# Projecting every token chunk with the activations as TensorE weights

## The chip, the cores and the metric

The kernel runs on one core of one Trainium2 chip. Its metric is the device time in microseconds (us) of one execution. TensorE (PE in the profile, PEld for its weight loads), VectorE (DVE), ScalarE (ACT), GpSimd (POOL) and the DMA queues of SyncE (SP), ACT and POOL run side by side, each through its own list of instructions in a fixed order, and wait for one another by semaphores.

## The reference

Two stages follow one another: a linear attention with a second-order feature map, and a feed-forward layer with a rational activation.

```python
# q, k, v: [4, 4, 1088, 32] (batch, head, sequence, head_dim); S1, S2: [8, 32]
def phi(x):                                   # 64 features per token and head
    a = einsum('rd,bhsd->bhsr', S1, x)
    b = einsum('rd,bhsd->bhsr', S2, x)
    return einsum('bhsi,bhsj->bhsij', a, b).reshape(..., 64)
q_p, k_p = phi(q), phi(k)
kv = einsum('bhsf,bhsd->bhfd', k_p, v)
z  = k_p.sum(axis=2)
x  = einsum('bhsf,bhfd->bhsd', q_p, kv) / (einsum('bhsf,bhf->bhs', q_p, z)[..., None] + 1e-6)
x  = x.transpose(0, 2, 1, 3).reshape(4352, 128)
# w_in: [128, 2048], w_out: [2048, 128], a: [4], b: [2]
h = x @ w_in
P = a[0] + a[1]*h + a[2]*h**2 + a[3]*h**3
Q = 1 + abs(b[0])*abs(h) + abs(b[1])*h**2
out = (P / (Q + 1e-6)) @ w_out                # [4352, 128], float32
```

## The kernel before

**Tiling.** The 4352 tokens are cut into ten chunks. The 4 x 1024 tokens of the main part give chunk `0` (128 tokens), chunk `0b` (384) and chunks `1` to `7` (512 each); the last 64 tokens of the four batches together are chunk `8` (256 tokens, the remainder). In the code `n` counts them from 0 to 9, and `lab(n)` gives the label. The 2048 hidden units are 16 blocks of 128 (`fi`). A group is one chunk with some of its blocks: chunk `0` has groups 0, 1, 2 (4, 4 and 8 blocks), chunk `0b` groups 3 and 4, chunks `1` to `7` two groups of 8 blocks each (5 to 18), the remainder groups 19 to 22 (8, 4, 3 and 1 blocks).

**One group** (`add_group`). TensorE computes `h` in float32 into `h_ps` (two buffers); ACT, and for some groups DVE, copies it to bf16 (`hev`, tile `hb`). DVE forms |h| (`abs`, tile `u`) and h squared (`sq`, tile `lin`). Q is u plus lin (`+Q`), added by an accumulating DMA of the POOL queue for groups 3 to 19 and by DVE otherwise. ACT takes the logarithm (`ln`, tile `L`) and the exponential of its negative (`exp`, back to `u`), which gives 1/Q. DVE builds the numerator in `y` (`odd`, `oddt`, then `+P`, by DMA or DVE) and multiplies it by 1/Q (`n5`). TensorE projects `y` with `w_out_b` into one PSUM bank, `out_ps` (`py`); for groups 11 to 22, whose plan has a "z", it also projects 1/Q itself with `w_out_0` (`pr`).

**The projection** (`project`). For nine of the ten chunks the weights are a 128x128 block of `w_out` and the chunk's `y` columns move (L891): 16 matmuls a chunk, or 32 with `pr`. The result lies with the output features on the partitions. So ACT copies it to SBUF (`oev`, L896, tile `o_sb`), TensorE transposes it in blocks of 128 tokens (`otr`, L901), ACT copies the transposes to `oT` (`otev`, L906), and SP stores that. The remainder alone (`BY_TOKEN = (9,)`) goes by tokens: a 128-token block of `y` is the weights and a block of `w_out` moves, 128 columns (L886); the result has tokens on the partitions, and one copy (L962) takes it to `oT`.

**Attention.** `add_keys(b)` makes the key features and the sums over them for batch b (`k tr`, `k ab`, `k prod`, `kv`, ...); `add_queries(n)` makes the chunk's attention output `xT` (`q tr`, `q abc`, `q dpr`: product for the denominator, `q prod`, `qp tr`, `x mm`, `x ev`). They share three PSUM buffers `w_ps` with `otr` and with the zeros below.

**Zeros.** `hot` multiplies zeros by zeros on TensorE, 23 matmuls of 512 columns in nine steps of `HOT` sizes (L1054), without effect on the output.

**Order.** Every piece is a step of `Plan`, with its engine, what it comes after, and the buffers that it takes and gives. `ORDER` is a list of the step numbers, written out, in which the steps are issued; each engine runs its share of them in that order. The costs given to `plan.add` have no effect while `ORDER` stands.

Of the kernel before, what the change touches and what calls it, by code (L numbers as in the profile page):

```python
# [55 lines left out]


class Plan:
# [66 lines left out]
def kernel(  # L125
# [14 lines left out]
    B, H, S, D = q.shape  # L140
# [7 lines left out]
    REM = S - MAIN  # L148
    JC = 4
    CW = JC * 128  # L150
# [9 lines left out]
    PLANS = {**{g: "QP" for g in range(4, 20)}, **{g:"QPz" for g in range(11,20)},5:"QP",3:"Q",4:"sQP",17:"Qz",20:"z",21:"z",22:"z"}  # L160
    CASTS = {18:(6,),16:(6,),14:(6,),12:(6,),17:(6,),13:(6,),15:(6,),11:(6,),10:(6,),9:(6,),8:(6,),7:(6,)}
    PACKED = (0, 9)
    BY_TOKEN = (9,)
    HOT = [1, 1, 1, 1, 5, 4, 6, 2, 2]
    ZEROS = 8
    assert d_model == 128 and H == 4 and D == 32 and R == 8 and REM == 64 and J % JC == 0

# [15 lines left out]
    plan = Plan(BUFS)  # L183
# [422 lines left out]
    def lab(n):  # L606
        return n - 1 if n > 1 else ("0", "0b")[n]
# [179 lines left out]
    def add_group(g, G):  # L787
        W, fis, n, how = G["W"], G["fis"], G["n"], G["how"]
        gw = W * len(fis)
        step = W if CW % W == 0 else CW  # L790
        subs = [(i, min(1024 // W, len(fis) - i)) for i in range(0, len(fis), 1024 // W)]
        by_token = n in BY_TOKEN
        final = fis[-1] == NF - 1
# [21 lines left out]
        def take(kind):  # L815
            return [] if packed else [KINDS[kind][0]]

        def got(kind):
            return [T[kind, "got", n]] if packed else []
# [88 lines left out]

        hes = []
        for s, nsub in subs:  # L910
            at = s * W // CW if W > B * REM or not by_token else s
            hm = plan.add("PE", 858 * nsub * W // 512, lambda s=s, w=nsub: h_mm(s, w), after=[G["x_step"], ld["wi"]], rank=g - 1.45,
                          take=["h_ps"], give=["xT"] if final and (s, nsub) == subs[-1] else [], name=f"h {g},{at}")
            dve = s in G["casts"]
            hes.append(plan.add("DVE" if dve else "ACT", 72 + nsub * W * 1.045 if dve else 32 + nsub * W * 0.853,
                                lambda s=s, w=nsub, e=nc.vector.tensor_copy if dve else nc.scalar.copy: h_evac(s, w, e), after=[hm] + got("t") + hes[:1], rank=g - 1.45,
                                take=take("t") if s == 0 else [], give=["h_ps"], name=f"hev {g},{at}"))
        pw = W // 128 * 85 if by_token else W / 2.4 + 3
        ts, tt = gw / 3.84 + 68, gw / 1.92 + 68

        def add_up(name, dst, src, after, rank, give=()):
# [23 lines left out]
        if z:  # L945
            rt = plan.add("PE", len(fis) * pw, lambda: project("u", w_out_0, first, False),
                          after=[e, rt] + c_w0[:1 + (fis[-1] >= NF // 2)], rank=g + 0.45, take=["out_ps"] if first else [], name=f"pr {g}")
# [11 lines left out]
        if final and by_token:  # L959
            def o_tokens():  # L960
                T["oT", n] = tile_of(moe, "oT", [128, JC, d_model], FP)
                nc.scalar.copy(out=T["oT", n][:, :W // 128, :],  # L962
                               in_=T["o", n][:, :W].rearrange("p (n d) -> p n d", d=d_model))

            t = plan.add("ACT", 32 + W * 109 // 128, o_tokens, after=[o], rank=g + 0.57, take=["oT"], give=["out_ps"],
                         name=f"otev {lab(n)}")
            t = plan.add("SP", 650, lambda: G["store"](T["oT", n]), after=[t], rank=g + 0.6, name=f"store {lab(n)}")
            plan.add("ST", 1, lambda: None, after=[t], rank=g + 0.6, give=["oT"], name=f"stored {lab(n)}")
        elif final:
            ev = 32 + W * 109 // 128  # L970
            o = plan.add("ACT", ev, o_evac, after=[o], rank=g + 0.56, take=["o_sb"], give=["out_ps"], name=f"oev {lab(n)}")
            t = plan.add("PE", 110 * (W // 128), o_transposes, after=[o], rank=g + 0.57, take=["w_ps"], give=["o_sb"],
                         name=f"otr {lab(n)}")
            t = plan.add("ACT", ev, oT_evac, after=[t], rank=g + 0.57, take=["oT"], give=["w_ps"], name=f"otev {lab(n)}")
            t = plan.add("SP", 650, lambda: G["store"](T["oT", n]), after=[t], rank=g + 0.6, name=f"store {lab(n)}")
            plan.add("ST", 1, lambda: None, after=[t], rank=g + 0.6, give=["oT"], lag=700, name=f"stored {lab(n)}")
# [32 lines left out]
    for n in range(len(chunks) + 1):  # L1009

        rank = first_of[n] - 2.6
        if n < len(chunks):
# [5 lines left out]
            def srcs(b=b, c=c, j0=j0, nj=nj):  # L1018
# [13 lines left out]
                give=["kq"] if c == NCH - 1 else [], early=early, pair=c if b > 0 else None)  # L1032
# [57 lines left out]
```

## Time and profile before

| what | value |
|---|---|
| median of 3 runs (lowest, highest) | 246.5 us (246.37, 246.71) |
| the profiled execution, its own time | 246.79 us |
| span, first to last instruction, in that execution | 244.8 us |
| PE busy | 237.0 us (97%), 1138 instructions |
| PEld busy | 137.0 us (56%), 1138 instructions |
| DVE busy | 223.8 us (91%), 241 instructions |
| ACT busy | 219.4 us (90%), 198 instructions |
| POOL busy | 50.1 us (20%), 70 instructions |
| mean granted TensorE clock | 0.998 |

A profile shows one execution. Busy time is the time in which an engine had at least one instruction under way; the modelled ends of pipelined matmuls overlap the next ones, so that for PE the distance from start to start says what a matmul costs. Engines are listed by line of the kernel (L891), with the tile written, an arrow and the tiles read. A figure in square brackets behind a row of a timeline is the time that the engine sat idle before it, and who ended that. The execution's own time is 2.0 us above its span.

### The profile page before, as it was taken

What the parts mean: (1) busy time and instruction counts of PE and PEld (TensorE: products, weight loads), DVE (VectorE), ACT (ScalarE), POOL (GpSimd) and SP (SyncE); (2) the same over time, 40 slices, a digit from 0 to 9 for tenths busy, and PEclk for the clock granted to TensorE, in tenths of its full rate; (3) what the DMA queues carried; (4) which work ended last, traced back from release to release, by engine and by line L of the source; (5) the groups of instructions that cost most, each with busy time, mean ns of one, the idle gap of its engine ahead of it and who ended that gap; (6) DMA issues with size and microseconds to landing.
All of it is one profiled execution on the core that took longest, in us unless ns stands there. A gap on an engine that the chain in (4) does not pass through costs nothing.

```text
span 244.8 us, 3043 instructions
## 1 busy us (share of the span) xinstructions
PE 237.0 (97%) x1138; PEld 137.0 (56%) x1138; DVE 223.8 (91%) x241; ACT 219.4 (90%) x198; POOL 50.1 (20%) x70
## 2 busy tenths in 40 slices
PE   8999999999999999999999999999999999999983
PEld 4888676655566555554554655344344444655452
DVE  0759969999999999999999999999999998999992
ACT  3337998998899979999999999999999999999993
POOL 7800020104021505030121420212211113111100
PEclk9999999999999999999999999999999999999999
DMA  6996716668959799989999899999999999999912
GB/s 165 277 319 170 255 22 111 166 135 196 188 99 185 126 183 181 188 158 191 205 173 184 151 212 187 187 209 183 189 189 215 185 175 181 203 190 179 194 43 67
DMA packets 22207, 42.96 MB, mean 175 GB/s; under 512 B 5537, under 2 KB 12721, under 8 KB 22065
## 3 DMA queue, kind: packets, MB, share of 16 engines
q0 software_dynamic: 8544, 31.74, 72.5%
q1 hardware_dynamic: 13360, 10.95, 14.9%
q8 instruction: 9, 0.15, 0.2%
q10 hardware_dynamic: 288, 0.08, 0.2%
q14 instruction: 6, 0.04, 0.0%
HBM read 8.82 MB, written 2.23 MB: 45 GB/s over the span
## 4 chain that ended last, share of the span: by engine, by line
PE 81%; DVE 8%; DMA 4%; ACT 4%; issue 2%; SPq 0%; DVEq 0%; ACTq 0%
PE h_ps L834 44%; PE out_ps L891 11%; PE w_ps L501 7%; DVE y L871 4%; PE w_ps L688 3%; PE w_ps L630 3%; PE w_ps L464 3%; PE w_ps L676 3%; DMA u<-lin 3%; PE w_ps L620 2%; ACT L L875 2%; DMA kq<-in_k_dram 2%; ACT u L878 2%; PE w_ps L455 1%; DVE lin L861 1%
## 5 line engine op out<-in xcount | busy, mean ns | idle before, releaser
L834 PE MATMUL h_ps<-xT,w_in_sb 128*128 128x512 f32 (+3 forms) x320 | 127.4, 534 | 0.0
L834 PEld LDWEIGHTS h_ps<-xT,w_in_sb 128*128 128x128 f32 x320 | 55.2, 190 | 42.1 <-issue 32.4
L875 ACT ACTIVATE L<-u,kappa 128x4096 f32<-128x4096 bf16 (+6 forms) x23 | 65.9, 2866 | 0.2 <-DMA u<-lin 0.2
L878 ACT ACTIVATE u<-L 128x4096 bf16<-128x4096 f32 (+6 forms) x23 | 63.7, 2769 | 0.1
L841 ACT CAST hb<-h_ps 128x1024 bf16<-128x1024 f32 (+3 forms) x52 | 52.1, 1022 | 5.1 <-PE h_ps L834 4.9
L927 POOL DMA_DIRECT2D u<-lin x17 | 21.1, 1241 | 115.8 <-DVE u L853 42.2
L871 DVE TENSOR_TENSOR y<-y,u 128x4096 bf16<-128x4096 bf16 (+6 forms) x23 | 39.6, 1727 | 1.1 <-ACT u L878 1.1
L871 DVE TENSOR_TENSOR y<-y,hb 128x4096 bf16<-128x4096 bf16 (+6 forms) x23 | 39.6, 1728 | 0.1
L861 DVE TENSOR_TENSOR lin<-hb 128x4096 bf16<-128x4096 bf16 (+6 forms) x22 | 38.0, 1728 | 0.7 <-ACT hb L841 0.6
L927 POOL DMA_DIRECT2D y<-lin x15 | 20.6, 1370 | 61.6 <-DVE lin L868 19.8
L891 PE MATMUL out_ps<-y,w_out_b 128*128 128x512 bf16 (+2 forms) x144 | 30.6, 355 | 0.9 <-DVE y L871 0.9
L865 DVE TENSOR_SCALAR y<-lin,a_t 128x4096 bf16<-128x4096 bf16 (+6 forms) x23 | 25.0, 1089 | 1.1 <-PE out_ps L891 0.9
L891 PEld LDWEIGHTS <-w_out_b 128*128 128x128 bf16 x144 | 13.3, 98 | 20.2 <-issue 7.9
L853 DVE TENSOR_SCALAR u<-hb 128x4096 int16<-128x4096 int16 (+6 forms) x23 | 21.6, 941 | 0.3 <-ACT hb L841 0.2
L891 PE MATMUL out_ps<-u,w_out 128*128 128x512 bf16 x64 | 15.1, 379 | 0.0
L841 DVE CAST hb<-h_ps 128x1024 bf16<-128x1024 f32 x12 | 14.6, 1214 | 0.0
L501 PEld LDWEIGHTS w_ps<-v_aug,k_p 128*128 128x128 f32 x112 | 13.4, 192 | 1.3 <-issue 1.0
L501 PE MATMUL w_ps<-v_aug,k_p 128*128 128x96 f32 x112 | 13.7, 274 | 0.0
L484 DVE TENSOR_TENSOR k_p<-ab 128x1024 f32<-128x1024 f32 x7 | 8.6, 1231 | 3.9 <-ACT q_pT L682 2.3
L891 PEld LDWEIGHTS <-w_out 128*128 128x128 bf16 x64 | 6.2, 98 | 8.4 <-issue 2.3
L868 DVE TENSOR_SCALAR lin<-lin,a_t 128x4096 bf16<-128x4096 bf16 (+3 forms) x11 | 10.9, 989 | 0.0
L676 PEld LDWEIGHTS w_ps<-ident,q_p 128*128 128x128 f32 x66 | 8.1, 141 | 5.0 <-issue 4.6
(121 smaller groups left out, 230.5 us busy)
## 6 DMA issues: line engine op xcount, KB each, us to landing
u<-lin POOLq DMA_DIRECT2D x14, 1024.0 KB, 9.4
y<-lin POOLq DMA_DIRECT2D x13, 1024.0 KB, 9.8
v_aug<-in_v_dram SPq DMA_DIRECT2D x8, 256.0 KB, 5.0
out_dram<-oT SPq DMA_DIRECT2D x7, 256.0 KB, 4.7
kq<-in_k_dram SPq DMA_DIRECT2D x3, 512.0 KB, 4.3
kq<-in_q_dram SPq DMA_DIRECT2D x3, 512.0 KB, 6.3
u<-lin POOLq DMA_DIRECT2D x2, 768.0 KB, 8.0
w_in_sb<-in_moe_w_in_dram SPq DMA_DIRECT2D x1, 1024.0 KB, 5.6
```

Source lines behind the costliest of these rows:

```text
L501: nc.tensor.matmul(kv_of((hp,))[:, 0], lhsT=lhs(hp), rhs=rhs(hp), start=(first and hp == hps[0]), stop=final, skip_group_check=True)
L676: nc.tensor.transpose(T["qpTp", n, hp][:, i * 128:(i + 1) * 128], in_=qp[:, i, hp * 128:(hp + 1) * 128], identity=ident)
L834: nc.tensor.matmul(T["h", g, s][:, i * step:i * step + W], lhsT=w_in_sb[:, fi * 128:(fi + 1) * 128], rhs=T["xT", n][:, :W], start=True, st ...
L841: copy(out=T["t", g][:, s * W:(s + nsub) * W], in_=T["h", g, s][:, :nsub * W])
L853: nc.vector.tensor_scalar(out=u().bitcast(mybir.dt.int16), in0=ht().bitcast(mybir.dt.int16), scalar1=0x7FFF, scalar2=None, op0=AX.bitwise_and)
L861: nc.vector.tensor_mul(out=sq(), in0=ht(), in1=ht())
L865: nc.vector.tensor_scalar(out=y(), in0=sq(), scalar1=a_t[:, 3:4], scalar2=a_t[:, 1:2], op0=AX.mult, op1=AX.add)
L871: return lambda: nc.vector.tensor_mul(out=out(), in0=in0(), in1=in1())
L875: nc.scalar.activation(out=T["L", g][:, :gw], in_=u(), func=ACT.Ln, bias=1.0 + 1e-6, scale=kappa[:, 2:3])
L878: nc.scalar.activation(out=u(), in_=T["L", g][:, :gw], func=ACT.Exp, scale=-1.0)
L891: nc.tensor.matmul(T["o", n][:, :W], lhsT=w[:, fi, :], rhs=T[src, g][:, i * W:(i + 1) * W], start=(start and i == 0), stop=(stop and i == ...
L927: nc.gpsimd.dma_start(out=dst(), in_=src(), accum_op=AX.add, max_dma_last_dim=GW)
```

## The change

All ten chunks go by tokens (`BY_TOKEN`). So for chunks `0` to `7` too `y` (and `u`, in `pr`) is loaded as weights in blocks of 128 tokens and a 128-column block of `w_out` moves; the copy `oev`, the transposes `otr` and the copy `otev` give way to one copy out of `out_ps` into `oT` (named `oev` for these chunks, the code of L962). The zeros are 26 matmuls instead of 23 and dealt out otherwise over the nine steps. `ORDER` is a new list, since there are 18 steps fewer and others are numbered anew. The rest of the diff changes costs and names.

```diff
 ORDER = [
-    ... (811 step numbers)
+    ... (793 step numbers in a new order)
-    BY_TOKEN = (9,)
-    HOT = [1, 1, 1, 1, 5, 4, 6, 2, 2]
+    BY_TOKEN = tuple(range(10))
+    HOT = [1, 1, 5, 8, 5, 1, 1, 2, 2]
...
-            at = s * W // CW if W > B * REM or not by_token else s
+            at = s if W == B * REM else s * W // CW
...
-        pw = W // 128 * 85 if by_token else W / 2.4 + 3
+        pw = W // 128 * 56 if by_token else W / 2.4 + 3
...
             t = plan.add("ACT", 32 + W * 109 // 128, o_tokens, after=[o], rank=g + 0.57, take=["oT"], give=["out_ps"],
-                         name=f"otev {lab(n)}")
+                         name=f"{'otev' if W == B * REM else 'oev'} {lab(n)}")
             t = plan.add("SP", 650, lambda: G["store"](T["oT", n]), after=[t], rank=g + 0.6, name=f"store {lab(n)}")
-            plan.add("ST", 1, lambda: None, after=[t], rank=g + 0.6, give=["oT"], name=f"stored {lab(n)}")
+            plan.add("ST", 1, lambda: None, after=[t], rank=g + 0.6, give=["oT"], lag=700, name=f"stored {lab(n)}")
```

The new order also moves work of the other stages. On DVE and ACT the opening is dealt anew. Until the first tile of h is there both orders are the same; then, where the old order went on with the query work of chunk 1, the new one first takes the pieces of chunk 0:

```
DVE before: sq 2, q dpr 1, odd 2, q dsum 1, abs 2, q dinv 1, q scale 1, q prod 1, oddt 2, abs 1, abs 0, ...
DVE after:  sq 2, w0 1, sq 0, abs 2, q dpr 1, abs 1, abs 0, odd 0, +Q 0, odd 2, q dsum 1, ... q prod 1, ...
PE before:  h 2, q abc 1, h 1, qp tr 0b, k tr 1, qp tr 0b, h 0, x mm 0b, ...
PE after:   h 2, h 0, k tr 1, qp tr 0b, h 1, qp tr 0b, q abc 1, x mm 0b, ...
ACT before: q eva 0b, q ev 1, hev 2, q eva 1, hev 1, qp ev 0b (twice), k ev 1, hev 0, x ev 0b, ...
ACT after:  q eva 0b, hev 2, q ev 1, hev 0, qp ev 0b (twice), k ev 1, hev 1, q eva 1, x ev 0b, ...
```

(`w0 1` scales half of `w_out` into `w_out_0`; `q ev`, `q eva`, `k ev`, `qp ev`, `x ev` are ACT's copies of the results of `q tr`, `q abc`, `k tr`, `qp tr`, `x mm`.)

In the closing part, from group 19 on, the order on DVE after is: sq 19, n5 17, odd 19, sq 20, oddt 19, sq 21, abs 20, abs 21, +Q 20, +Q 21, odd 21, n5 18, oddt 21, odd 20, abs 22, sq 22, oddt 20, +P 21, n5 19, +P 20, +Q 22, odd 22, n5 20, oddt 22, n5 21, +P 22, n5 22. On ACT it is: ln 18, exp 18, hev 22, ln 20, ln 19, exp 19, oev 7, ln 21, exp 20, exp 21, ln 22, exp 22 and the last copy.

65 rows, old and new, of the table ORDER are left out of this document.

## The prediction

> **What bounds the kernel now.** I read the page's busy times first, then busy time by stages, then the timelines of VectorE, TensorE and ScalarE at the places where something waits.
>
> ```profile
> PE 237.0 (97%) x1138; PEld 137.0 (56%) x1138; DVE 223.8 (91%) x241; ACT 219.4 (90%) x198; POOL 50.1 (20%) x70
> ```
> Three engines are above 90%, so the shares do not say which one sets the end. The stages say more. The columns are PE, PEld, DVE, ACT, POOL busy, each with its instructions, then granted clock, DMA share and GB/s.
>
> ```profile
> core 0: us, PE busy (x) PEld busy (x) DVE busy (x) ACT busy (x) POOL busy (x), PEclk, DMA share, GB/s
> 17.50:44.00 26.50, 26.50 (x164) 20.20 (x164) 23.47 (x43) 23.49 (x36) 1.53 (x2) 1.00 0.55 140
> 44.00:200.00 156.00, 156.00 (x643) 81.89 (x642) 154.62 (x125) 150.25 (x119) 32.11 (x25) 1.00 0.97 180
> 200.00:240.50 40.50, 38.37 (x229) 22.46 (x227) 38.18 (x39) 39.66 (x32) 7.16 (x6) 1.00 0.82 158
> ```
> In the long middle PE has no gap, DVE 1.38 us of idle time (156.00 - 154.62), ACT 5.75. In the closing part PE waits, while DVE has 2.32 us of idle time and ACT 0.84. So PE and DVE bind together up to 200 us, and DVE and ACT behind it. The change takes work from PE and from ACT and none from DVE: no line of DVE is in the diff, and its plans are the same. DVE's 223.8 us stay, and the time can fall by no more than DVE's waits. Those of some size are these, from the list of waits (us in total, times, longest):
>
> ```profile
> DVE k_p L484 <- ACT q_pT L682: 2.3, 1, 2.3
> ...
> DVE y L871 <- ACT u L878: 1.1, 3, 0.6
> DVE y L865 <- PE out_ps L891: 0.9, 2, 0.7
> ...
> DVE lin L861 <- ACT hb L841: 0.6, 2, 0.4
> ```
> The first lies in the opening and comes from the one `k_p` buffer: the product of batch 1's second half stands in DVE's list until PE has used the first half. The 1.1 us and the longest times of the last two rows, 0.7 and 0.4, lie in the closing part: `n5` waits for `exp`, `odd 17` for a `y` buffer that `py 14` still reads, and `sq 22` for its copy of h. Together they are 2.2 of the 2.32 us.
>
> **The change part by part: TensorE.** The two forms of the projection stand side by side in this trace, the new one in the remainder chunk.
>
> ```profile
> L891 PE MATMUL out_ps<-y,w_out_b x144: 219/379/390, 50.6 to 233.2; 128*128 128x512 bf16 x112, 128*128 128x128 bf16 x16, 128*128 128x384 bf16 x16
> L891 PE MATMUL out_ps<-u,w_out x64: 376/379/379, 168.7 to 230.9; 128*128 128x512 bf16 x64
> L886 PE MATMUL out_ps<-w_out,u x32: 216/219/229, 234.9 to 240.4; 128*128 128x128 bf16 x32
> ```
> These are the tile's matmuls with their least, median and greatest duration in ns. The weight loads of the new form, and the places in PE's timeline where each form runs in a row:
>
> ```profile
> L886 PEld LDWEIGHTS <-u x32: 95/98/98, 234.4 to 240.3; 128*128 128x128 bf16 x32
> ```
> ```profile
> 206.65 1.89 PE L891 MATMUL out_ps<-u,w_out 128*128 128x512 bf16 x8
> 208.37 1.89 PE L891 MATMUL out_ps<-y,w_out_b 128*128 128x512 bf16 x8
> ...
> 222.67 0.60 PE L901 MATMUL w_ps<-ident,o_sb 128*128 128x128 f32 x4
> 223.10 1.89 PE L891 MATMUL out_ps<-u,w_out 128*128 128x512 bf16 x8
> ...
> 234.91 1.05 PE L886 MATMUL out_ps<-w_out,u 128*128 128x128 bf16 x16 [0.44 <-ACT o_sb L896]
> ```
> Old form: 208.37 - 206.65 = 1.72 us for 8 matmuls, 215 ns each. New form: 16 matmuls cover 1.05 us, of which the last one takes 0.22, so (1.05 - 0.22) / 15 = 55 ns each: the 98-ns weight loads lie under the matmuls before them. Four of these, 222 ns, take the place of one of 215 ns. The 112 + 64 matmuls of 512 columns become 704 of 128, and chunk `0b`'s 16 of 384 become 48; chunk `0` keeps 16. At 7 ns per block of 512 that adds 176 x 7 = 1.2 us, 1.3 with `0b`. The transposes go: four take 223.10 - 222.67 = 0.43 us, 32 of them 3.5. Three more zeros add 0.6. PE's sum is 1.3 - 3.5 + 0.6 = -1.6 us.
>
> The skill speaks against this step. The Trainium skill, page "TensorE: Matmul & The Clock Gate", section "Back-to-back issue gap", gives about 81 ns for each matmul of 128 columns in a stream of weight loads and matmuls, and about 131 ns for 512 columns. By that, 768 matmuls would cost (81 - 55) x 768 = 20 us more than I count. The 55 and 215 ns measured here agree with neither of its figures, and I take them.
>
> One more cost of the new form: `y` is the weights, so the first load of a group has to wait for `n5`, where a load of `w_out` could go ahead. It is nothing while `n5` is done before PE comes to the group; with PE ahead it is one 98-ns load for each group that waits, on PE, which has the 1.6 us to cover it.
>
> **ScalarE.** Per chunk there were two copies and there is one.
>
> ```profile
> L896 ACT COPY o_sb<-out_ps 128x512 f32<-128x512 f32 x7 | 4.6, 661 | 0.5 <-PE out_ps L891 0.5
> L906 ACT COPY oT<-w_ps 128x512 f32<-128x512 f32 x7 | 4.2, 599 | 0.0
> ```
> The seven large ones of a kind take 4.2 us busy, the two small ones below 1: about 4.5 us less for ACT. The 0.2 or so by which its copies overlap could make it 4.
>
> **VectorE: where the new order makes it wait.** Terms here are changes of DVE's idle time, since its work stays. First the opening, with rows of PE, ACT and DVE in turn:
>
> ```profile
> 16.84 1.98 PE L834 MATMUL h_ps<-xT,w_in_sb 128*128 128x128 f32 x16
> 18.65 1.03 PE L630 MATMUL w_ps<-W_abc,qT 128*128 128x96 f32 x8
> ```
> ```profile
> 17.38 0.59 ACT L624 COPY qT<-w_ps 128x512 f32<-128x512 f32 x1
> 18.85 1.01 ACT L841 CAST hb<-h_ps 128x1024 bf16<-128x1024 f32 x1 [0.88 <-PE h_ps L834]
> 19.76 0.48 ACT L640 COPY abc<-w_ps 128x384 f32<-128x384 f32 x1
> ...
> 39.72 2.77 ACT L859 ACTIVATE lin<-hb 128x3072 bf16<-128x3072 bf16 x1
> ```
> ```profile
> 19.90 0.69 DVE L861 TENSOR_TENSOR lin<-hb 128x1024 bf16<-128x1024 bf16 x1 [0.27 <-ACT hb L841]
> 20.51 0.29 DVE L651 TENSOR_TENSOR den<-abc 128x128 f32<-128x128 f32 x1
> ...
> 26.33 0.75 DVE L437 TENSOR_SCALAR w_out<-y,a_sb 128x1024 bf16<-128x1024 f32 x1
> ```
> Before, `q abc 1` runs at 18.65, right behind h 2. After, PE first does h 0 (half of h 2's 1.81, so 0.9), seven transposes (0.11 each, 0.8), h 1 (0.9) and three more transposes (0.3): `q abc 1` starts at about 21.6 and ends 0.9 later, at 22.5. On ACT `q eva 1` then stands behind `k ev 1` and `hev 1`, two copies of up to 0.6 us like the one at 17.38, and ends near 23.6. DVE, after `sq 2` at 19.90, has only half of `w_out`, `sq 0` and `abs 2` ahead of `q dpr 1`, 0.6 + 0.7 us and twice about 0.4 (they are shorter than `sq 2`): it is free at 21.9 or so and waits 1.7 us. Behind `q dpr 1` are queued `abs 1`, `abs 0`, `odd 0` and all that follows. Near 43 us a second wait comes: on ACT `exp 2` now stands behind the 2.77-us square of group 4 and behind `exp 0`, `ln 2` and two copies, and DVE's `n5 2` is due first, by about 1.0 us. The old 2.3 us go, because `kv 1` on PE and the second product on DVE both come later than in the old order and `w0 0`, `abs 4` and `+P 2` stand between the two products. So 2.3 us give way to 2.7: +0.4. Bounds: the 2.3 stay as well, +2.7; only the 1.0 comes, -1.3.
>
> In the middle I leave DVE's 1.38 us as they are. PE's 1.6 us become waits of PE for `h_ps` buffers that DVE empties, and ACT's 4 us become waits for h and for the accumulating DMAs. Bounds: -1.0 us (most of the idle goes) to +1.0 (for instance `n5 5`, which has moved closer behind its `+P` landing).
>
> In the closing part the waits for ACT and for `y` go if ACT keeps ahead. The tightest chain is `+Q 19` by DMA, `ln 19`, `exp 19`, `n5 19`.
>
> ```profile
> 223.02 2.28 DVE L871 TENSOR_TENSOR y<-y,u 128x4096 bf16<-128x4096 bf16 x1
> ...
> 235.11 1.22 DVE L871 TENSOR_TENSOR y<-y,u 128x2048 bf16<-128x2048 bf16 x1
> ```
> ```profile
> 230.44 2.00 ACT L875 ACTIVATE L<-u,kappa 128x2048 f32<-128x2048 bf16 x1 [0.20 <-DMA u<-lin]
> 232.47 1.91 ACT L878 ACTIVATE u<-L 128x2048 bf16<-128x2048 f32 x1
> ```
> From `n5 17` (223.02) to `n5 19` (235.11) DVE did the same pieces as it does after, apart from the two short ones of group 22 (an estimate of 0.4, from `sq 2`'s 0.69 for four times their width and a fixed part): 12.1 us less the longest wait for `exp` (0.6) plus 0.4 = 11.9 us. The chain from 223.02 to the end of `exp 19` (234.38) is 11.4. So `n5 19` comes when its data are there. Group 22's square and absolute value now lie ahead of it, and the copies `otev 5` and `otev 7` are gone from ACT's last stretch. Of the 2.2 us of waits in this part I take -1.4, since 0.5 us of margin is little. Bounds: -2.2 and 0. Behind the last `n5` nothing changes: two matmuls, a copy, a store.
>
> The sum: +0.4 + 0 - 1.4 = -1.0 us. For the profiled execution that is 246.8 - 1.0 = 245.8 us; the median of the runs stands 0.3 below it, so the forecast is 246.5 - 1.0 = 245.5 us.
>
> **The rivals.** *The opening starves VectorE* (slower): the wait at `q dpr 1` costs more than 1.7 us, or the old 2.3 us remain as well, and DVE, which has no slack to win it back in 156 us, carries it to the end. At +2.7 in the opening and the -1.4 of the closing part it is 246.5 + 1.3 = 247.8 us; it decides once the opening's waits exceed the old 3.0 (26.50 - 23.47) by more than the 1.4 of the closing part. For it: every number there hangs on copies of ACT in sequence. Against it: the work moved ahead (h 0, half of `w_out`) is work that DVE need not do later. Chance 0.24.
>
> *Nothing to be seen*: opening and closing part cancel, 246.5 us within 0.5. That is 0.2%, about what a measurement of this kernel can tell from no change. For it: DVE's work is the same to the instruction. Chance 0.15.
>
> *More gain*: one of the opening's two new waits stays away (the longer one: +0.4 - 1.7 = -1.3), and the closing part gives what I count: -1.3 - 1.4 = -2.7, 243.8 us. For it: ACT has 4 us more of slack than I use. Chance 0.15.
>
> *Weight loads not hidden* (much slower): in groups of 32 the loads set the pace at their 98 ns. 768 x (98 - 55) = 33 us on PE, less 2.9 for transposes and zeros, on an engine without a gap up to 200 us: about 276 us. Against it: the run of 16 at 55 ns. Chance 0.03. By the 81 ns of the Trainium skill's page on TensorE, named above, it would be about 264 us.
>
> **How the numbers follow.** The forecast, between 0.5 and 1.8 us faster, has what is left, 0.43. Faster by over 0.2%: 0.43 + 0.15 = 0.58; within it 0.15; slower 0.24 + 0.03 = 0.27. The likeliest time is 245.5 us. The range goes from the gain case to the starved one, each with half of the middle part's bound (0.5): 243.8 - 0.5 = 243.3 to 247.8 + 0.5 = 248.3 us. It leaves out the ends of both and the last rival. The forecast's own range is 244.7 to 246.0.
>
> **What would show it.** In the profile after, the new matmuls should lie 55 to 57 ns apart, PE should show waits in the middle, and ACT about 215 us busy, DVE 224. DVE should wait 1 to 2 us before the denominator product of chunk 1 near 22 us, and no longer before `k_p` at 36. After 200 us DVE's idle time should be below 1.2 us. The forecast is wrong if DVE's idle time in the opening is above 5 us, if waits of DVE for h appear between 44 and 200 us, or if the matmuls are 80 ns apart or more.

## The result, and the profile after

| | before | after |
|---|---|---|
| median of 5 runs (lowest, highest) | 246.71 us (246.37, 246.96) | 245.16 us (244.98, 245.95) |
| the profiled execution, its own time | 246.79 us | 245.12 us |
| its span | 244.8 us | 243.0 us |

After against before is 0.9948, 95% interval 0.9934 to 0.9961: 1.55 us less by the medians. The busy times, from the page of after:

```profile
PE 235.4 (97%) x1665; PEld 158.0 (65%) x1669; DVE 222.5 (92%) x241; ACT 215.4 (89%) x189; POOL 50.7 (21%) x70
```
PE has 1.6 us less than in before, ACT 4.0 less, and DVE 1.3 less, with the same 241 instructions. The same three stages as in the prediction (PE, PEld, DVE, ACT, POOL busy, clock, DMA share, GB/s); the last is cut where DVE's last `n5` ends, 1.8 us earlier than in before:

```profile
17.50:44.00 26.50, 26.50 (x159) 19.76 (x158) 23.33 (x43) 22.17 (x34) 3.79 (x2) 1.00 0.59 148
44.00:200.00 156.00, 155.57 (x1004) 97.06 (x1004) 154.16 (x124) 149.87 (x117) 32.26 (x25) 1.00 0.97 180
200.00:238.70 38.70, 36.22 (x398) 28.00 (x399) 37.49 (x39) 37.47 (x26) 5.29 (x5) 1.00 0.86 167
```
DVE's idle time is 3.17, 1.84 and 1.21 us; in before it was 3.03, 1.38 and 2.32. That is 0.5 us less, and with the 1.3 us of busy time it makes the 1.8 us by which the spans of these two executions differ. DVE's waits of some size, from the list of waits of after:

```profile
DVE den L650 <- ACT abc L639: 3.4, 2, 1.7
DVE k_p L483 <- ACT ab L470: 1.8, 1, 1.8
DVE y L870 <- DMA y<-lin: 1.0, 1, 1.0
DVE y L870 <- ACT u L877: 0.7, 1, 0.7
DVE hb L840 <- PE h_ps L833: 0.4, 2, 0.2
```
One of the first row's two waits, and the second row's, lie ahead of 17.5 us, in both kernels. The others in DVE's timeline, with the product that no longer waits (39.26) and, behind `n5 15`, `odd 17`:

```profile
23.62 0.29 DVE L650 TENSOR_TENSOR den<-abc 128x128 f32<-128x128 f32 x1 [1.71 <-ACT abc L639]
...
30.49 1.76 DVE L860 TENSOR_TENSOR lin<-hb 128x3072 bf16<-128x3072 bf16 x1 [0.23 <-ACT hb L842]
...
39.26 1.22 DVE L483 TENSOR_TENSOR k_p<-ab 128x1024 f32<-128x1024 f32 x1
...
44.30 0.69 DVE L870 TENSOR_TENSOR y<-y,u 128x1024 bf16<-128x1024 bf16 x1 [0.71 <-ACT u L877]
...
203.96 2.29 DVE L870 TENSOR_TENSOR y<-y,u 128x4096 bf16<-128x4096 bf16 x1 [0.96 <-DMA y<-lin]
206.17 1.34 DVE L864 TENSOR_SCALAR y<-lin,a_t 128x4096 bf16<-128x4096 bf16 x1
```
The wait ahead of `q dpr 1` (23.62) and the one ahead of `n5 2` (44.30) came, and the old one at `k_p` went. New is the 0.96 us at `n5 15`, which waits for the landing of `+P 15`.

The chain that ended last, of before and then of after:

```profile
PE 81%; DVE 8%; DMA 4%; ACT 4%; issue 2%; SPq 0%; DVEq 0%; ACTq 0%
```
```profile
PE 71%; DVE 18%; issue 5%; DMA 4%; ACT 0%; DVEq 0%
```
It runs through PE for most of the time. In before it leaves PE near 202.6 us, in after much earlier, here:

```profile
169.79 1.79 PE h_ps L833 x4
...
171.60 1.22 DVE hb L840
...
192.66 0.61 DVE y L870
193.28 10.59 DMA y<-lin
```
This reading was not weighed in the prediction, and it gives a rival: PE paces the kernel, and the 1.6 us taken from PE are the 1.55 us won. The experiments begin there.

### The profile page after: what moved, and what is told of

It is laid out like the page before. It is cut to its first block, busy times and chain, and to the rows that moved or that the text cites. A ratio compares the mean times of both kernels' runs of the same rounds, so it can differ in the third digit from the quotient of the medians.

```text
span 243.0 us, 4086 instructions
## 1 busy us (share of the span) xinstructions
PE 235.4 (97%) x1665; PEld 158.0 (65%) x1669; DVE 222.5 (92%) x241; ACT 215.4 (89%) x189; POOL 50.7 (21%) x70
## 4 chain that ended last, share of the span: by engine, by line
PE 71%; DVE 18%; issue 5%; DMA 4%; ACT 0%; DVEq 0%
PE h_ps L833 38%; DVE y L870 9%; PE out_ps L885 8%; PE w_ps L500 7%; DMA y<-lin 4%; PE w_ps L463 3%; PE w_ps L629 3%; PE w_ps L687 3%; PE w_ps L675 3%; DVE y L864 2%; DVE lin L860 2%; PE w_ps L454 2%; PE w_ps L619 2%; PE out_ps L359 1%; DVE y L922 1%
## 5 line engine op out<-in xcount | busy, mean ns | idle before, releaser
L877 ACT ACTIVATE u<-L 128x4096 bf16<-128x4096 f32 (+6 forms) x23 | 62.9, 2745 | 0.1
L840 ACT CAST hb<-h_ps 128x1024 bf16<-128x1024 f32 (+3 forms) x52 | 51.3, 999 | 4.5 <-PE h_ps L833 4.2
L926 POOL DMA_DIRECT2D u<-lin x17 | 22.4, 1315 | 105.7 <-DVE u L852 44.4
L885 PEld LDWEIGHTS <-y 128*128 128x128 bf16 x544 | 31.8, 98 | 7.7 <-DVE y L870 3.6
L885 PE MATMUL out_ps<-w_out_b,y 128*128 128x128 bf16 x544 | 34.2, 219 | 2.1 <-DVE y L870 2.0
L926 POOL DMA_DIRECT2D y<-lin x15 | 19.0, 1265 | 70.7 <-DVE lin L867 23.9
L885 PEld LDWEIGHTS <-u 128*128 128x128 bf16 x288 | 16.8, 98 | 3.4 <-issue 2.5
L885 PE MATMUL out_ps<-w_out,u 128*128 128x128 bf16 x288 | 18.1, 219 | 0.3 <-ACT oT L961 0.2
L681 ACT COPY q_pT<-w_ps 128x512 f32<-128x512 f32 (+2 forms) x18 | 10.3, 581 | 0.9 <-PE w_ps L675 0.9
L667 DVE TENSOR_TENSOR q_p<-abc 128x1024 f32<-128x1024 f32 (+3 forms) x10 | 10.6, 1064 | 0.1
```

Of the source, the lines that this page charges most:

```text
L840: copy(out=T["t", g][:, s * W:(s + nsub) * W], in_=T["h", g, s][:, :nsub * W])
L877: nc.scalar.activation(out=u(), in_=T["L", g][:, :gw], func=ACT.Exp, scale=-1.0)
L885: nc.tensor.matmul(T["o", n][:, k * 128:(k + 1) * 128], lhsT=T[src, g][:, i * W + k * 128:i * W + (k + 1) * 128], rhs=w[:, fi, :], start=( ...
L926: nc.gpsimd.dma_start(out=dst(), in_=src(), accum_op=AX.add, max_dma_last_dim=GW)
```

## The experiments

Ratios are against before, run in the same rounds on the same chip; after itself was not run again in these rounds. Where a kernel is set against after, the difference of the two ratios times 246.7 us is given; by the two intervals it is uncertain by 0.4 to 0.6 us. Where the medians say something else, that is added.

| kernel | median | ratio, 95% interval |
|---|---|---|
| after | 245.16 us | 0.9948, 0.9934 to 0.9961 |
| new form, old order, old zeros | 246.46 us | 0.9995, 0.9985 to 1.0005 |
| old form, new order, new zeros | 248.99 us | 1.0095, 1.0082 to 1.0108 |
| after, zeros dealt as before | 246.26 us | 0.9977, 0.9967 to 0.9988 |
| after, no zeros | 244.87 us | 0.9927, 0.9908 to 0.9947 |
| after, opening's wait filled | 245.17 us | 0.9941, 0.9922 to 0.9961 |
| after, wait at `n5 15` filled | 245.06 us | 0.9929, 0.9911 to 0.9946 |
| after, PE +3.4 us | 247.82 us | 1.0055, 1.0041 to 1.0070 |
| after, PE -3.6 us | 244.66 us | 0.9906, 0.9887 to 0.9926 |
| after, DVE +2.3 us | 247.07 us | 1.0007, 0.9996 to 1.0018 |
| after, ACT +3 us, 59 to 187 us | 245.82 us | 0.9956, 0.9939 to 0.9973 |
| after, ACT +1.6 us, 200 to 235 us | 246.44 us | 0.9980, 0.9966 to 0.9994 |
| before, PE +3.4 us | 249.78 us | 1.0117, 1.0098 to 1.0136 |

**The form alone.** After's code, before's order without the `otr` and `otev` steps, before's zeros:

```diff
-    HOT = [1, 1, 5, 8, 5, 1, 1, 2, 2]
+    HOT = [1, 1, 1, 1, 5, 4, 6, 2, 2]
-ORDER = [... (after's)]
+ORDER = [... (before's, less otr and otev)]
```


> The new form of the projection in the order and with the zeros of before: each step keeps its place in the old order, the two transposing steps of each chunk fall out, the one copy stands where the first copy stood. PE's work falls by 2.2 us against before (the prediction's 1.6, and the 0.6 of three zeros that are not added), ACT's by 4.2. Theory D (VectorE's waits set the time; what PE and ACT save counts only as far as a wait of DVE goes): the 2.3-us wait at k_p stays, some of the closing part's 2.2 us go, so -0.5 us against before (0 to -1.5), about 246.2 us, ratio 0.998. Theory P (TensorE, which has no gap up to 200 us and holds most of the chain that ended last, sets the time; the 1.6 us that the whole change took from PE are the 1.55 us that it won): -2.2 us, about 244.5 us, ratio 0.991.

0.9995: nothing, 0.1 us within 0.25. Theory P is out for this order; of theory D's half a microsecond little or nothing came, and the 2.3-us wait at `k_p` stayed (2.27). The first two stages of this kernel, and one late `odd` of the long middle in this kernel and in before:

```profile
17.50:44.00 26.50, 26.50 (x164) 20.20 (x163) 23.47 (x43) 23.49 (x36) 1.54 (x2) 1.00 0.55 139
44.00:200.00 156.00, 155.70 (x973) 94.78 (x972) 154.77 (x125) 149.29 (x115) 32.93 (x26) 1.00 0.97 182
```
```profile
146.90 1.34 DVE L863 TENSOR_SCALAR y<-lin,a_t 128x4096 bf16<-128x4096 bf16 x1
```
```profile
146.97 1.34 DVE L865 TENSOR_SCALAR y<-lin,a_t 128x4096 bf16<-128x4096 bf16 x1
```
DVE's busy time in the opening is 23.47 us as in before, and at 147 us DVE stands within 0.07 us of before, though PE and ACT have had less to do. So in the old order lighter neighbours do not help DVE there; it goes at the pace of its own list.

**The order alone.** Before's code with after's order and zeros; each chunk's transposes and second copy put back a few steps behind its first copy.

```diff
-    HOT = [1, 1, 1, 1, 5, 4, 6, 2, 2]
+    HOT = [1, 1, 5, 8, 5, 1, 1, 2, 2]
-ORDER = [... (before's)]
+ORDER = [... (after's, with otr and otev put in)]
```


> The old form of the projection (two copies and four transposes per chunk) in the order and with the zeros of after: every step stands as in after, and each chunk's transposes and second copy are put a few steps behind its first copy. PE's work is before's plus 0.6 us of zeros, ACT's is before's. Theory D: the opening's waits come out as in after (3.2 us), the closing part is better than in before by less than in after: between 245.5 and 247, 246.2 us, ratio 0.998. Theory P: before's time plus the zeros, 247.3 us, ratio 1.002 or above. If it is slower by more than 1 us, the order of after is made for the lighter ScalarE and neither half of the change brings the gain alone.

2.3 us slower than before, the last of the three outcomes. The two rows that cost most, ACT's and DVE's:

```profile
209.11 0.59 ACT L905 COPY oT<-w_ps 128x512 f32<-128x512 f32 x1 [1.71 <-PE w_ps L900]
```
```profile
210.64 2.29 DVE L860 TENSOR_TENSOR lin<-hb 128x4096 bf16<-128x4096 bf16 x1 [2.91 <-ACT hb L840]
```
A copy of the old form waits for its transposes on PE, and behind it on ACT stands the copy of h that `sq 18` waits for. Where these steps were put back was my choice, so the size depends on that; a better place was not tried. That the order alone would be no gain is shown for this placement only.

**The zeros.** First the old deal in after's order, then none at all. (Theory H, which the run at `n5 15` below spells out, has TensorE pace the kernel up to about 171 us and VectorE behind that; the runs stand here by subject, not in the order in which they were made.)

```diff
-    HOT = [1, 1, 5, 8, 5, 1, 1, 2, 2]
+    HOT = [1, 1, 1, 1, 5, 4, 6, 2, 2]
```


> After, with the zeros dealt as in before (1, 1, 1, 1, 5, 4, 6, 2, 2 in place of 1, 1, 5, 8, 5, 1, 1, 2, 2; the steps stay where they are): the part of the change that deals them anew, undone alone. Theory H: no difference, 245.2 us, ratio 0.994, up to +0.3 where six zeros now stand ahead of a projection. Theory Z: 0.5 us longer or more, where fewer zeros fill the waits at 223 and 227 us.

```diff
-        for _ in range(n):
+        for _ in range(0):
```


> After, without the 26 zero matmuls (their results are read by nobody; the steps stay, empty): 5.6 us of TensorE's work less, nearly all of it after 223 us, where TensorE waits for VectorE. Theory H: they lie in TensorE's waits, 0 to -0.3 us, 245.0 us, ratio 0.993. Theory Z (the zeros hold TensorE at its rate): the granted clock falls below 1.00 or the last projections' matmuls lie further apart than 55.8 ns, 0.5 to 2 us longer, ratio 0.996 to 1.002. Theory P: TensorE paces the end as well, -1 us or more, ratio below 0.990.

With the old deal it is 0.7 us slower than after (1.1 by the medians): theory H's 0 was wrong. In this order the steps with 4 and 6 zeros follow each other directly, ahead of the remainder's projections. PE in this run, then PE and two windows in the run without zeros:

```profile
20.07 0.65 PE L454 MATMUL w_ps<-ident,kq 128*128 128x128 f32 x4 [0.52 <-DMA kq<-in_k_dram]
...
234.62 2.35 PE L1053 MATMUL w_ps<-const-float32-0.0 128*128 128x512 bf16 x9
236.81 1.05 PE L885 MATMUL out_ps<-w_out,u 128*128 128x128 bf16 x16
```
```profile
228.84 1.96 PE L885 MATMUL out_ps<-w_out,u 128*128 128x128 bf16 x32 [1.80 <-ACT u L877]
```
```profile
221.00:229.00 8.00, 4.46 (x69) 3.82 (x68) 8.00 (x10) 7.97 (x4) 1.74 (x2) 1.00 0.96 193
240.00:243.00 3.00, 0.00 (x0) 0.00 (x0) 0.00 (x0) 0.00 (x0) 0.00 (x0) 0.70 0.20 44
```
The first projection behind them starts at 236.81 us, in after at 234.87. Of these 1.94 us some 0.6 have nothing to do with the zeros: in this one execution PE waited 0.52 us near 20 us for a load of keys, and at 204 us DVE was already 0.58 us behind after. The rest, 1.4 us, is close to the 1.7 us of the eight zeros more (0.215 us each) that stand there. Without zeros the time is the same as after's within the error (0.5 us less by the ratios, 0.3 by the medians), the clock stays at 1.00 through a wait of 1.80 us, and the 32 matmuls behind it still take 1.96 us. So in this order the zeros win nothing that can be measured, and where they stand can cost. Before was not run without its zeros, so what a better place for them alone would have given the old order is open. The Trainium skill, page "TensorE: Matmul & The Clock Gate", section "What's actually happening", puts the fall to half clock behind an idle window of about 3.4 us; no run here left PE idle for that long in this stage, so none shows it there. Behind the end of PE's work the fall is seen, and sooner: in the run without zeros the last matmul ends at 238.99 us, and the clock's mean of 0.70 from 240 to 243 us comes of a fall to 0.5 at 241.2 us, 2.2 us later. So 1.80 us did no harm here, but the margin is not shown to be wide.

**The opening's wait filled.** Only DVE's order is changed.

```diff
-DVE: abs 2, q dpr 1, abs 1, abs 0, odd 0, +Q 0, odd 2, q dsum 1, ... oddt 0, ...
+DVE: abs 2, abs 0, odd 0, +Q 0, odd 2, oddt 0, q dpr 1, abs 1, q dsum 1, ...
```


> After, with one edit of VectorE's order alone: abs 0, odd 0, +Q 0, odd 2 and oddt 0, whose data are there, are moved ahead of q dpr 1, where DVE waits 1.71 us for ScalarE. No work is added or taken away, PE and ACT keep their lists. Theory D: the wait is filled, and DVE ends 1.3 to 1.7 us earlier: 243.7 us, ratio 0.988. Theory P: TensorE's list is the same, so the time stays at 245.2 us, ratio 0.994.

Nothing: 0.2 us less by the ratios, none by the medians. DVE and, below, ACT and PE in this run:

```profile
23.32 0.42 DVE L869 TENSOR_TENSOR y<-y,hb 128x512 bf16<-128x512 bf16 x1
23.76 0.29 DVE L649 TENSOR_TENSOR den<-abc 128x128 f32<-128x128 f32 x1
...
30.63 1.76 DVE L859 TENSOR_TENSOR lin<-hb 128x3072 bf16<-128x3072 bf16 x1 [1.88 <-ACT hb L841]
```
```profile
27.22 0.80 ACT L841 CAST hb<-h_ps 128x768 bf16<-128x768 f32 x1 [0.49 <-PE h_ps L832]
...
29.80 0.80 ACT L841 CAST hb<-h_ps 128x768 bf16<-128x768 f32 x1 [0.22 <-PE h_ps L832]
```
```profile
24.39 5.38 PE L832 MATMUL h_ps<-xT,w_in_sb 128*128 128x384 f32 x16
```
The 1.71 us are gone from `q dpr 1`, and 1.88 us stand at `sq 3`, where after has 0.23. `sq 3` needs h 3, ACT's copies of h 3 wait for PE up to the last one (29.80), and PE's 16 matmuls of h 3 take the same 5.38 us as in after without a gap. So PE paces this stage of after, and DVE's wait there is a symptom: it moves to the next place where DVE meets PE. This speaks for theory P and against theory D.

**The wait at `n5 15` filled.** The same kind of edit late.

```diff
-DVE: hev 18,6, n5 15, odd 17, sq 18, ...
+DVE: hev 18,6, odd 17, n5 15, sq 18, ...
```


> After, with one edit of VectorE's order alone: odd 17 (1.34 us, its data are there) is moved ahead of n5 15, where DVE waits 0.96 us for the landing of +P 15 near 204 us. It is the same kind of edit as in the run that filled the opening's wait, in the other stage. Theory H (handover: TensorE paces after's order from the opening to about 171 us, VectorE paces it from there to the end, with one transfer between): the wait is filled where DVE paces, -0.9 us, 244.3 us, ratio 0.990. Theory P (TensorE paces all the way): 245.2 us, ratio 0.994. Theory D (VectorE's waits set the time everywhere) gives -0.9 us too, but is already spoken against by the opening.

0.5 us less by the ratios, 0.1 by the medians; the intervals of after and of this run overlap, so no gain is shown. In the profile the 0.96 us come back elsewhere:

```profile
203.10 1.34 DVE L863 TENSOR_SCALAR y<-lin,a_t 128x4096 bf16<-128x4096 bf16 x1
204.35 2.29 DVE L869 TENSOR_TENSOR y<-y,u 128x4096 bf16<-128x4096 bf16 x1
207.04 2.29 DVE L859 TENSOR_TENSOR lin<-hb 128x4096 bf16<-128x4096 bf16 x1 [0.40 <-ACT hb L839]
...
216.68 2.29 DVE L869 TENSOR_TENSOR y<-y,u 128x4096 bf16<-128x4096 bf16 x1 [0.43 <-ACT hb L839]
```
`n5 15` no longer waits, and two new waits of 0.40 and 0.43 us for ACT take the place of 0.96: `sq 18` and `n5 16`. Here ACT is as far along as DVE, so theory H's handover to VectorE alone is too simple as well.

**Work put on or taken off one engine at a time.** PE first, in after and in before; the same edit in both:

```diff
-            for i in range(nsub):
+            for i in ([0] if s == 2 and g in (7, 10, 13, 16) else []) + list(range(nsub)):
                 fi = fis[s + i]
```


> After, with four matmuls of 512 columns in the middle done twice (the first of the second h block of groups 7, 10, 13 and 16, 0.43 us each): PE gets back 1.7 us of work there, as much as the change took from it. Theory D: PE's slack takes them, 245.2 to 245.6 us, ratio 0.994 to 0.996. Theory P: 1.7 us longer, 246.9 us, ratio 1.001.

> Before, with the same four matmuls done twice as in the earlier run on after (in the trace each is two records of 0.43 us, so that edit added 3.4 us, not 1.7, and after became 2.65 us longer). Theory H: in the old order VectorE and TensorE pace together, as the run of the new form in the old order says (VectorE's instructions start at the same times as in before up to 147 us, though TensorE has less to do), so the cost is as large as in after or larger: 2.6 to 3.4 us, 249.2 to 250.1 us, ratio 1.011 to 1.014. If VectorE alone paces the old order and TensorE has room, the cost is below 1.5 us, ratio below 1.006.

The first text gives the edit half its size: each repeated matmul is two records of 0.43 us, so PE gets 3.4 us, not 1.7. After becomes 2.6 us longer by the ratios, before 2.9. In after, DVE's waits for h, which were 0.4 us in total, become

```profile
DVE hb L840 <- PE h_ps L833: 2.6, 5, 1.0
```
and these 2.2 us more are most of the loss. In before PE has no more room than in after, although in the run of the form alone a lighter PE won nothing there: PE and DVE run level in the old order.

PE lightened, and DVE loaded:

```diff
             for i, fi in enumerate(fis):
+                if src == "y" and g in (6, 8, 10, 12) and 2 <= i < 6:
+                    continue
```


> After, with half of the rows left out of the y projection of groups 6, 8, 10 and 12 (their sums are then not the reference's): 64 matmuls of 55.8 ns less, 3.6 us of TensorE's work in the stretch that it paces. Theory P: -3.6 us, 241.6 us, ratio 0.980. Theory H: VectorE is right behind TensorE and takes over the pace, so the gain is no more than its waits there: -0.3 to -1.0, 244.5 us, ratio 0.991. Theory D: nothing, 245.2 us, ratio 0.994.

```diff
             nc.vector.tensor_scalar(out=u().bitcast(mybir.dt.int16), in0=ht().bitcast(mybir.dt.int16),
                                     scalar1=0x7FFF, scalar2=None, op0=AX.bitwise_and)
+            if g in (8, 13):
+                nc.vector.tensor_scalar(out=u().bitcast(mybir.dt.int16), in0=ht().bitcast(mybir.dt.int16),
+                                        scalar1=0x7FFF, scalar2=None, op0=AX.bitwise_and)
```


> After, with the absolute value of groups 8 and 13 done twice (1.22 us each, 1.14 as they overlap): DVE has 2.3 us more work in the stretch that TensorE paces. Theory D: 2.3 us longer, 247.5 us, ratio 1.004. Theory P: TensorE's list is the same, up to 0.3 us longer, 245.2 to 245.5 us, ratio 0.994 to 0.995. Theory H: DVE follows TensorE with little room (0.4 us of waits for h in the middle), so most of it shows: +1.3 to +2.3, 246.5 us or more, ratio 1.000 to 1.004.

3.6 us less on PE bring 1.0 us by the ratios (0.5 by the medians); 2.3 us more on DVE cost 1.5 (1.9). The long middle in the run with less on PE, one of PE's rows there, and two waits that grow in this run; then the middle in the run with more on DVE:

```profile
44.00:200.00 156.00, 154.53 (x947) 94.02 (x945) 154.39 (x124) 150.38 (x119) 32.14 (x25) 1.00 0.97 181
```
```profile
154.74 1.09 PE L675 MATMUL w_ps<-ident,q_p 128*128 128x128 f32 x8 [0.62 <-DVE q_p L667]
```
```profile
DVE y L870 <- ACT u L877: 1.8, 3, 0.7
...
PE out_ps L887 <- ACT u L877: 1.8, 1, 1.8
```
```profile
44.00:200.00 156.00, 154.59 (x977) 95.37 (x976) 154.50 (x124) 148.28 (x117) 31.10 (x24) 1.00 0.95 178
```
In both, PE has 1.4 to 1.5 us of gaps in the middle, where after has 0.4. With more on DVE they are waits for DVE; with less on PE 0.62 us are, and the rest are waits for copies by ACT. What is new in the two waits listed, for `exp`, lies in the closing part. So neither engine has much room beside the other in the middle, as theory H expected of these two runs and P and D did not.

ScalarE, with the copy out of PSUM done twice, for the first six chunks (`n < 6`, shown) and, in another kernel, for the next three (`n in (6, 7, 8)`):

```diff
                 nc.scalar.copy(out=T["oT", n][:, :W // 128, :],
                                in_=T["o", n][:, :W].rearrange("p (n d) -> p n d", d=d_model))
+                if n < 6:
+                    nc.scalar.copy(out=T["oT", n][:, :W // 128, :],
+                                   in_=T["o", n][:, :W].rearrange("p (n d) -> p n d", d=d_model))
```


> After, with the copy out of PSUM done twice for chunks 0, 0b, 1, 2, 3 and 4 (0.30, 0.50 and four of about 0.59 us, at 59 to 187 us): ScalarE gets back 3 us of the work that the change took from it, in the stretch that TensorE and VectorE pace together. Theory H: ScalarE has room there (149.87 of 156 us busy), 0 to +0.5 us, 245.2 to 245.7 us, ratio 0.994 to 0.996. Theory A (the gain is ScalarE's, everywhere): +3, 248.2 us, ratio 1.006.

> After, with the copy out of PSUM done twice for chunks 5, 6 and 7 (three of 0.59 us, at 200, 221 and 234 us): ScalarE gets back 1.6 us (with the overlap) in the closing part, where from 206 us it has no gap of more than 0.2 us up to 238. Theory H: the three engines are level there, so most of it shows: +1.0 to +1.6, 246.2 to 246.8 us, ratio 0.998 to 1.001. If VectorE alone paced the closing part, 0 to +0.3, ratio 0.994 to 0.995.

3 us in the long stretch cost 0.2 us by the ratios (0.7 by the medians), about what the error covers; 1.6 us in the closing part cost 0.8 within 0.5 (1.3 by the medians). PE in the second run:

```profile
230.14 1.96 PE L885 MATMUL out_ps<-w_out,u 128*128 128x128 bf16 x32 [0.67 <-ACT u L877]
...
236.37 1.05 PE L885 MATMUL out_ps<-w_out,u 128*128 128x128 bf16 x16 [0.96 <-ACT oT L964]
```
PE waits for `exp 18` and for the copy ahead of the remainder's first projection. So ACT's work counts in the closing part, and little or not at all before it.

## Why the prediction came out as it did

The forecast was 245.5 us, the median is 245.16. The sign and the size hold; the working behind them holds in part, and that the number came so close is in part luck. The forecast was 1.0 us less idle time on DVE at the same work. In the profiles DVE's idle time fell by 0.5 us only, and the other 1.3 of the 1.8 us stand in a term that was held fixed.

**TensorE.** Right in size. One of the many rows:

```profile
205.62 1.95 PE L885 MATMUL out_ps<-w_out,u 128*128 128x128 bf16 x32
```
(1.95 - 0.22) / 31 = 55.8 ns each, 55 were taken, and PE's sum is the -1.6 us worked out. The 81 ns of the Trainium skill, page "TensorE: Matmul & The Clock Gate", section "Back-to-back issue gap", do not hold for this stream; the same page of the Trainium skill has, in its section "Wait — 56ns, not 53.3ns?", 55.6 and 215.7 ns, which fit the 55.8 measured here and the 215 of the old form. Wrong was what PE would do with the 1.6 us: they were to become PE's waits for `h_ps` buffers in the middle. PE has 0.43 us of gaps there, mostly for `xT`, and over the whole run the waits of its weight loads for copies out of `h_ps` fell, from 3.7 us in before to 2.7. Instead DVE waited for h, twice between 44 and 200 us, 0.17 and 0.21 us: the prediction had named such waits as a sign that it is wrong. They are short.

**ScalarE.** The -4.0 us came (219.4 to 215.4). They were counted as slack; in the closing part about half of a load put on ACT was time, so a saving there may be too.

**VectorE's work.** "DVE's 223.8 us stay, and the time can fall by no more than DVE's waits": this is the step that failed. The instructions are the same, but their busy time fell by 1.3 us. The `odd` of full width in before and in after, 14 each, and one such instruction of before:

```profile
L865 DVE TENSOR_SCALAR y<-lin,a_t 128x4096 bf16<-128x4096 bf16 x14 | 19.4, 1383 | 1.1 <-PE out_ps L891 0.9
```
```profile
L864 DVE TENSOR_SCALAR y<-lin,a_t 128x4096 bf16<-128x4096 bf16 x14 | 18.7, 1338 | 0.2 <-PE out_ps L885 0.2
```
```profile
202.61 1.64 DVE L865 TENSOR_SCALAR y<-lin,a_t 128x4096 bf16<-128x4096 bf16 x1 [0.68 <-PE out_ps L891]
```
The slow `odd` of 1.64 us, one of 1.58 and one of 1.44 in before, against 1.34 in after, are 0.7 us of it. The wait ahead of it does not explain the slow one: in before with more on PE an `odd` ran 1.35 us behind a wait of 1.05, and the one of 1.58 had no wait. Other instructions are a little longer in after, by 0.3 us in all. The rest, 1.0 us, is overlap: an instruction that waits for nothing starts some 0.08 us before the one ahead of it ends. By the starts and durations in the traces these overlaps are 15.5 us in before and 16.5 in after, since four more pairs overlap, and each by 0.003 us more. What can be said is that the fall goes with the order. DVE's busy time is 223.4 to 224.6 us in the three kernels with the old order and 222.3 to 223.0 in the ten with the new one and no more work on DVE; the old form in the new order has 222.9. Why, no run here shows.

**The opening.** Every wait named there came about as worked out: 1.71 us at `q dpr 1` (1.7), 0.71 at `n5 2` (1.0), none at `k_p`. The idle time up to 44 us grew by 0.1 us, and 0.3 of the wait at `n5 2` lie behind that cut: together the +0.4 taken. But as a term of the sum the 1.71 us are worth nothing, as filling them showed: PE, not the order on DVE, sets when `sq 3` can start. Waits of one engine are not terms that add up while another engine paces.

**The middle and the closing part.** The middle's idle time grew by 0.5 us, 0.3 of them that rest of the wait at `n5 2` (taken: 0, within ±1.0). The closing part gave 1.1 us of idle time (taken: 1.4, below 1.2 left; 1.21 is left), in spite of the 0.96 us at `n5 15`, which the prediction had not seen.

**The zeros.** "Three more zeros add 0.6" counted their work and not their place. Their new deal is worth 0.7 us in the new order (within 0.4). The new list also issues them later: of the three that before has ahead of 200 us (166.34, 187.32 and 198.08 us) two stand in the closing part in after, 0.4 us of PE's work less in the middle, which no run tried alone.

**The rivals.** The opening did not starve DVE (3.17 us, against the 3.03 and 1.4 more that it needed), the weight loads stayed hidden (55.8 ns a matmul against their 98), "nothing to be seen" is ruled out by the interval (0.9961 at most), and the gain is between the forecast and the greater one.

What the runs show in place of "DVE's waits set the time": up to about 170 us PE and DVE are level within a microsecond or so, and in the closing part ACT with them. The form gave nothing alone, and the new order with the old form lost 2.3 us in the one placement tried. With the new form the new order won 0.4 us (0.9995 to 0.9977) and the new deal of zeros another 0.7 (to 0.9948), each within 0.4; all together gave 1.55 us. So the form took work from PE and ACT, and a new order was needed to make time of it. How much of that belongs to which step of the order was not taken apart. No version tried here beats after by more than the error.

## What to carry to other kernels

When three engines are above 90%, the longest wait in the list is not what a cure of it would win: load or lighten each engine by a known amount in a known stage, and see what share arrives (here, by the ratios, 0.8 of PE's load, 0.6 of DVE's, 0.3 of PE's relief, 0.5 of ACT's load at the end and 0.1 before; each within 0.2, ACT's at the end within 0.3). A lighter form and an order made for it have to be tried together; each of them alone can show nothing or a loss. Filler work has its place in the order like other work, and has to be placed anew, or left out, when the order changes.

## What was not expected of the hardware

One instruction of VectorE in before ran 0.30 us longer than its like (1.64 against 1.34 us), in the same place in before with more on PE too; why, no run here shows. And the start is not fixed: the same product of the opening (`q dpr 0b`), ahead of any difference between the kernels in this study, began between 17.36 and 18.00 us in the fourteen profiles, so two profiles that differ by half a microsecond may differ there. Before's and after's, at 17.51 and 17.50, do not.
